# Attention and a gated MLP in one kernel: the opening reordered, weight joins and masks interleaved, the gate rewritten

## The chip, the cores and the metric

One core of a Trainium2 chip runs the whole program. The metric is device time in microseconds (us) from one launch to its end; the kernel before was timed three times, and one execution of it was profiled.

## The reference

Inputs are q, k, v of 4 batches, 8 heads, 768 positions, 64 dimensions, and two float64 weight matrices w_in (512 x 2048) and w_out (2048 x 512). Cut to what is computed:

```python
k_sum = k.reshape(B, H, nb, 32, D).max(axis=3)        # one summary key per block of 32
v_sum = v.reshape(B, H, nb, 32, D).mean(axis=3)
scores_l = scale * q @ k.T, masked to |i - j| < 16
scores_s = scale * q @ k_sum.T + log(32)
a = softmax(concat([scores_l, scores_s]))             # float32
x = (a @ concat([v, v_sum])) laid out as (3072, 512)
h = x @ w_in                                          # (3072, 2048)
g = where(h >= 1, h, where(h <= -1, 0, (h + 1)**2 / 4))
out = (g @ w_out).astype(float32)
```

## The kernel before

The 3072 rows of x are cut into 8 chunks of T = 384 (chunk c is half c % 2 of batch c // 2). For each chunk, attention runs over 4 head pairs p. Then the MLP runs over 16 blocks f of 128 hidden columns: `ff1` (F) makes h, the gate (G, H, I) makes t, `gate_high` (J) and `gate_rest` (O) split t into a high and a low part, and `ff2` (B) adds t @ w_out into three accumulators. Every product of the MLP is made of three matmuls on high and low halves, so F is 12 matmuls and B is 9.

A step has a letter and digits: `S13` is the scores of chunk 1, pair 3, `F0a2` the third part of ff1 of chunk 0, block 10. The attention letters are: r, k, q, y, v loads (raw keys, windowed keys, queries, raw values, windowed values); R, Y sums over blocks; K, C keys put together; S scores; M mask and row maximum; E exps; D reciprocals; N norms; T transposes and P their copies out of PSUM; Z, V, W the summary values; A the product with the values; X and L its high and low half. The dictionary `steps` maps them to functions.

The weights arrive as float64 words and are converted on the chip, in 16 pairs of pieces. Pair i holds w_out block i-1 and w_in block i+1 (pair 0: w_in blocks 0 and 1; pair 15: w_out blocks 14 and 15), so F of block f needs pair f-1 and B of block f needs pair f+1. A pair goes through w (fetch, 1 MB by two DMAs), a and b (two scalings on ScalarE), c (the join: shift, merge and add on VectorE through a PSUM bank, two halves of 512 columns), d (rounding to the high half) and e (the low half, on GpSimd). `HI_POOL` lists the pairs whose d runs on GpSimd; the others run on ScalarE.

The order is written out by hand for the opening only: the string `OPENING` is the order of all steps of chunk 0, of the attention of chunk 1 and of the start of chunk 2, and each engine gets its instructions in that order. After it a loop emits F, G, H, I, J, O of block f, one attention step of the next chunk, and B of block f-2 (LAG = 2); a scheduler places those. h has two PSUM banks (`ps_h`), so F of block f+2 can start only once the gate has read h of block f for the last time. All other PSUM tiles share six banks (`ps`), of which the accumulators hold three. Raw keys, raw values and joined weights share three buffers (`W_BUFS`). Loads are all issued in order by SyncE, with eight in flight.

Of the kernel before, what the change touches and what calls it, by code (L numbers as in the profile page):

```python
# [40 lines left out]
D001 T000 y01 Y01 a0 c00 c01 P000 N001 T001 P001 q01 S01 M011 M010 w1 a1 b1 y02 Y02 E011 D011 q02 S02 M021 M020 C03
q03 S03 v00 v01 V00 W00 v02 N011 k10 w2 E010 D010 N010 y03 Z01 Z02 V01 W01 V02 W02 c10 q10 q11 E021 D021 N021 E020
D020 N020 v03 C10 A00 T010 M030 P010 T011 M031 P011 v10 X00 L00 b2 Y03 E030 D030 N030 k11 C11 A01 T021 P021 X01 L01
v11 T020 P020 S10 M100 M101 q12 E031 D031 N031 E100 D100 N100 Z03 V03 W03 Z10 V10 W10 S11 q13 c11 E101 D101 N101 a2
A02 X02 T030 M110 T031 P031 M111 L02 E110 D110 E111 D111 N111 N110 k12 k13 C13 C12 P030 d0 d1 e0 e1 Z11 Z12 V11 W11
c20 c21 A03 X03 T101 P101 T100 L03 P100 w3 w4 a3 w5 b3 A10 X10 T110 P110 T111 P111 L10 v12 S12 M120 M121 q20 k20 S13
q21 E120 M131 M130 D120 N120 E121 k21 E131 D131 N131 D121 N121 V12 W12 F000 F001 F010 F011 F012 F002 F003 G00 F013
E130 D130 N130 G01 b4 c30 c31 H01 A11 T121 X11 L11 P121 T120 P120 I01 H00 I00 a4 a5 w6 w7 w8 a6 d2 e2 J00 O00 Z13 d3
e3 A12 T131 T130 P131 P130 c40 c41 d4 e4 F020 F030 F031 F032 F021 F022 F023 G02 F033 B00 b5 b6 v13 V13 W13 c50 v20
H02 I02 F040 F041 F042 F043 b7 b8 J01 O01 J02 O02 B01 B02 w9 b9 wa ba c51 c60 d5 e5 G03 H03 G04 c61 d6 H04 I04 F050  # L50
F051 F052 F053 I03 F060 F061 F062 a7 c70 c71 a8 a9 aa c80 F063 J03 O03 B03 G05 J04 O04 B04 G06 X12 e6 L12 d7 e7 H05
I05 F070 J05 F071 F072 F073 c81 d8 e8 H06 I06 J06 F080 F081 F082 F083 wb bb ab wc bc wd we wf bd be bf c90 c91 d9 ca0
A13 v21 O05 G07 H07 B05 O06 B06 G08 H08 ca1 e9 I07 F090 F091 F092 F093 I08 F0a0 F0a1 F0a2 F0a3 cb0 cb1 J07 O07 G09
B07 J08 O08 G0a B08 ac cc0 ad ae af H0a I0a da db ea F0b0 F0b1 eb F0b2 F0b3 H09 I09 F0c0 F0c1 F0c2 F0c3 cc1 cd0 cd1
J09 J0a O09 G0b O0a G0c H0b I0b B09 B0a H0c I0c dc ec F0d0 F0d1 F0d2 F0d3 dd ed F0e0 F0e1 F0e2 F0e3 ce0 ce1 cf0 J0b
J0c O0b O0c G0d H0d G0e H0e B0b B0c cf1 de df ee ef I0e F0f0 F0f1 F0f2 F0f3 I0d F100 F101 F102 J0d J0e X13 L13 F103
O0d O0e B0d G0f H0f I0f F110 F111 F112 F113 G10 H10 I10 F120 F121 F122 F123 B0e r20 R20 C20 y21 Y21 r21 R21 C21 J0f
J10 O0f G11 H11 B0f
# [8 lines left out]
def fused_kernel(ctx: ExitStack, tc: tile.TileContext, q2, kT, kwin, vT, vwin, w_in, w_out, mask, ident, out):  # L67
# [167 lines left out]
    def masks(c, p, j):  # L235
        e = es[c, p, j] = att.tile([P, NT, KA], F32, tag=f"e{j}", name=f"e{c}_{p}_{j}", bufs=E_BUFS)
        at = c % NHALF
        nc.vector.scalar_tensor_tensor(  # L238
            out=e, in0=s_pss[c, p][j][:, :NT * KA].rearrange("p (t n) -> p t n", n=KA), scalar=1.0 / math.sqrt(D),
            in1=mask_sb[:, at:at + NT], op0=ALU.mult, op1=ALU.add)  # L240
        dens[c, p, j] = att.tile([P, 2, NT], F32, tag=f"den{j}", name=f"den{c}_{p}_{j}")
        nc.vector.tensor_reduce(out=dens[c, p, j][:, 0], in_=e, axis=AX.X, op=ALU.max, negate=True)  # L242
# [214 lines left out]
```

## Time and profile before

| quantity | value |
| --- | --- |
| timed runs | 686.19 us median of 3 (685.07 to 1181.96) |
| profiled execution | 684.8 us |
| its span, first to last instruction | 683.0 us |
| TensorE (PE) busy | 641.8 us, 94% of the span |
| VectorE (DVE), ScalarE (ACT), GpSimd (POOL) busy | 338.6, 312.4, 260.2 us |
| mean granted TensorE clock | 0.988 |

The median and the profiled execution belong together; the 1181.96 us is one disturbed run. The span leaves 1.8 us of the profiled time outside. PE is the engine to watch: where it is busy all the time, no other engine matters. Some matmul records can be missing from a trace.

### The profile page before, as it was taken

The numbers are of one execution on the slowest core, as the hardware profiler recorded it, in microseconds if no ns is written. First come the engines' busy times: TensorE is split into PE (matmuls) and PEld (weight loads), VectorE is DVE, ScalarE is ACT, GpSimd is POOL, SyncE is SP. The second block draws the span as 40 slices with busy tenths as digits, with TensorE's granted clock in tenths as the row PEclk, the third lists the DMA queues.
The fourth block names the chain that finished last, engine by engine and source line by source line (L and its number), as shares of the span: only waits on it lengthen the run. The fifth ranks groups of instructions, "written<-read, shape, count | busy, mean of one in ns | idle before, by whom it ended". The sixth has DMA issues, their size and how long they took to land.

```text
span 683.0 us, 11672 instructions
## 1 busy us (share of the span) xinstructions
PE 641.8 (94%) x4448; PEld 558.9 (82%) x4448; DVE 338.6 (50%) x689; ACT 312.4 (46%) x825; POOL 260.2 (38%) x292
## 2 busy tenths in 40 slices
...
GB/s 309 324 242 343 341 166 0 50 139 151 64 63 55 118 63 46 62 119 191 63 45 37 155 46 63 63 65 246 31 50 62 93 63 18 1 1 46 1 1 46
DMA packets 31399, 69.05 MB, mean 101 GB/s; under 512 B 2928, under 2 KB 11376, under 8 KB 31344
## 3 DMA queue, kind: packets, MB, share of 16 engines
...
q8 instruction: 35, 0.57, 0.4%
...
HBM read 62.01 MB, written 6.29 MB: 100 GB/s over the span
## 4 chain that ended last, share of the span: by engine, by line
PE 82%; DMA 8%; DVE 6%; issue 2%; SPq 1%; ACT 1%; POOL 0%; DVEq 0%; POOLq 0%; ACTq 0%
PE acc L325 37%; PE h L294 35%; PE o_ps L273 4%; PE s_ps L231 3%; DMA raw<-in_w_out 3%; PE t_ps L262 3%; DMA raw<-in_w_in 3%; DVE c L127 2%; DMA first<-in_vT 1%; DVE c L125 1%; DVE w L129 1%; DMA first<-in_kT 1%; DVE t L300 1%; DVE t L306 1%; SPq L101 1%
## 5 line engine op out<-in xcount | busy, mean ns | idle before, releaser
L294 PE MATMUL h<-xhi,halves 128*128 128x384 f32 x1024 | 283.1, 339 | 7.0 <-DVE t L306 6.4
L316 POOL TENSOR_TENSOR glo<-t,ghi 128x384 fp32r<-128x384 f32 x128 | 129.7, 1016 | 329.3 <-PE acc L325 177.4
L325 PE MATMUL acc<-halves,ghi 128*128 128x512 f32 x768 | 240.6, 394 | 0.0
L294 PEld LDWEIGHTS h<-xhi,halves 128*128 128x128 f32 x1024 | 187.7, 188 | 14.4 <-DVE t L306 5.9
L303 ACT ACTIVATE t<-t,ones_half 128x384 f32<-128x384 f32 x128 | 78.6, 618 | 215.5 <-DVE t L300 215.3
L300 DVE TENSOR_SCALAR t<-h 128x384 f32<-128x384 f32 x128 | 70.6, 556 | 212.6 <-PE h L294 156.4
L294 PE MATMUL h<-xlo,halves 128*128 128x384 f32 x512 | 173.1, 338 | 0.0
L325 PEld LDWEIGHTS acc<-halves,ghi 128*128 128x128 f32 x768 | 144.8, 189 | 29.0
L325 PE MATMUL acc<-halves,glo 128*128 128x512 f32 x384 | 161.0, 419 | 1.3 <-POOL glo L316 1.3
L306 DVE TENSOR_TENSOR t<-h,t 128x384 f32<-128x384 f32 x128 | 70.8, 556 | 61.3 <-ACT t L303 61.0
L294 PEld LDWEIGHTS h<-xlo,halves 128*128 128x128 f32 x512 | 96.2, 188 | 5.1
L311 ACT CAST ghi<-t 128x384 fp32r<-128x384 f32 x128 | 65.2, 514 | 60.2 <-DVE t L306 57.1
L325 PEld LDWEIGHTS acc<-halves,glo 128*128 128x128 f32 x384 | 72.2, 188 | 20.8 <-issue 3.5
L247 ACT ACTIVATE e<-e,den 128x120 f32<-128x120 f32 x192 | 73.2, 383 | 17.7 <-DVE den L242 17.6
L257 POOL TENSOR_TENSOR e<-e,den 128x360 f32<-128x360 f32 x64 | 50.2, 790 | 29.6 <-DVE den L253 21.3
L266 ACT COPY pt<-t_ps 120x384 f32<-120x384 f32 x64 | 30.0, 474 | 48.9 <-PE t_ps L262 48.9
L142 POOL TENSOR_TENSOR halves<-w,halves 128x1024 fp32r<-128x1024 f32 x16 | 38.4, 2403 | 13.0 <-ACT halves L136 12.5
L231 PE MATMUL s_ps<-k,q 64*64 64x120 f32 x720 | 28.3, 294 | 12.0 <-DMA q<-in_q 6.8
L262 PE MATMUL t_ps<-ident_sb,e 128*120 128x128 f32 x192 | 30.8, 301 | 7.8 <-POOL e L257 7.8
L231 PEld LDWEIGHTS s_ps<-k,q 64*64 64x64 f32 x720 | 21.1, 147 | 19.6 <-POOL k L203 11.1
L238 DVE SCALAR_TENSOR_TENSOR e<-s_ps,mask_sb 128x360 f32<-128x360 f32 x64 | 33.4, 527 | 6.7 <-PE t_ps L262 3.0
L247 ACT ACTIVATION_READ_ACCUMULATOR e<-e,den 128x1 f32 x192 | 35.9, 187 | 0.0
...
## 6 DMA issues: line engine op xcount, KB each, us to landing
q<-in_q SPq DMA_DIRECT2D x30, 384.0 KB, 3.9
k<-in_kwin SPq DMA_DIRECT2D x28, 360.0 KB, 3.2
...
raw<-in_w_in SPq DMA_DIRECT2D x16, 512.0 KB, 10.3
raw<-in_w_out SPq DMA_DIRECT2D x16, 512.0 KB, 10.5
...
vraw<-in_vT SPq DMA_DIRECT2D x13, 384.0 KB, 3.5
kraw<-in_kT SPq DMA_DIRECT2D x13, 384.0 KB, 3.6
```

What stands on the lines that cost most here:

```text
L142: nc.gpsimd.tensor_tensor(out=lo, in0=converting[i].bitcast(F32), in1=hi.bitcast(F32), op=ALU.subtract)
L231: nc.tensor.matmul(s_ps[j][i * QB:(i + 1) * QB, t * KA:(t + 1) * KA], q_t[rows, blk, rows], k_t[rows, blk, :], start=True, stop=True)
L247: nc.scalar.activation(out=e[:, t, :], in_=e[:, t, :], func=AF.Exp, bias=nm[:, t:t + 1], scale=1.0, accum_out=den[:, t:t + 1])
L257: nc.gpsimd.tensor_tensor(out=e, in0=e, in1=den.unsqueeze(2).broadcast_to([P, NT, KA]), op=ALU.mult)
L262: nc.tensor.transpose(t_pss[c, p, j][:KA, t * P:(t + 1) * P], es[c, p, j][:, t, :], ident_sb)
L294: nc.tensor.matmul(hs[c, f][:, :T], weight["win", f][w][:, k * P:(k + 1) * P], x, start=(k == 0 and n == 0), stop=(k == NK - 1 and n == 2))
L300: nc.vector.tensor_scalar(out=ts[c, f], in0=hs[c, f][:, :T], scalar1=-1.0, scalar2=1.0, op0=ALU.max, op1=ALU.min)
L303: nc.scalar.activation(out=ts[c, f], in_=ts[c, f], func=AF.Square, bias=ones_half, scale=0.5)
L306: nc.vector.tensor_tensor(out=ts[c, f], in0=hs[c, f][:, :T], in1=ts[c, f], op=ALU.max)
L311: nc.scalar.copy(out=hi, in_=ts[c, f])
L316: nc.gpsimd.tensor_tensor(out=lo, in0=ts[c, f], in1=hi.bitcast(F32), op=ALU.subtract)
L325: nc.tensor.matmul(acc[c][i], a[:, rows], weight["wout", f][w], start=(f == 0 and n == 0), stop=(f == NF - 1 and n == 2))
```

## The change

Five things change, nothing in what is computed.

1. `convert_join` does both halves of a pair in one step. It takes two PSUM banks and issues shift, shift, merge, merge, add, add, where it issued shift, merge, add for one half and later the same for the other.
2. `masks` does both heads of a pair in one step: mask, mask, maximum, maximum instead of mask, maximum, mask, maximum.
3. The gate is written as min(r², max(h, 1)) with r = relu(h/2 + 1/2). The clip of h on DVE is gone; in its place ACT reads h from PSUM (relu with scale and bias), ACT squares, and DVE does max and min in one instruction.
4. `HI_POOL` holds all 16 pairs, so all d run on GpSimd.
5. `OPENING` is another order of the same steps.

```diff
-HI_POOL = [0, 2, 4, 6, 8, 10, 12, 14]
+HI_POOL = [0, 1, 2, 3, 4, 5, 6, 7, 8, 9, 10, 11, 12, 13, 14, 15]
...
 OPENING = """
-y00 Y00 r00 R00 K00 C00 q00 S00 r02 R02 m M001 M000 E000 Z00 r01 R01 w0 K01 C01 K02 C02 D000 N000 E001 r03 K03 R03 b0
+r03 r00 R00 r01 R01 K00 r02 q00 q01 m q02 q03 R03 K01 K02 C01 y02 C00 R02 C02 S00 S01 K03 C03 y00 w0 M00 E000 S02 M01
...
-        c_ps = ps.tile([P, DM], I32, tag="ps", name=f"c{i}_{part}")
-        nc.vector.tensor_scalar(out=c_ps, in0=top[:, cols], scalar1=3, scalar2=0x7FFFFFF8,
-                                op0=ALU.logical_shift_left, op1=ALU.bitwise_and)
-        nc.vector.scalar_tensor_tensor(out=c_ps, in0=top[:, cols], scalar=-0x80000000, in1=c_ps,
-                                       op0=ALU.bitwise_and, op1=ALU.bitwise_or)
-        nc.vector.tensor_tensor(out=w[:, cols], in0=c_ps, in1=low[:, cols], op=ALU.add)
+        c_ps = [ps.tile([P, DM], I32, tag="ps", name=f"c{i}_{part}") for part in range(2)]
+        cols = [slice(part * DM, (part + 1) * DM) for part in range(2)]
+        for part in range(2):
+            nc.vector.tensor_scalar(out=c_ps[part], in0=top[:, cols[part]], scalar1=3, scalar2=0x7FFFFFF8,
+                                    op0=ALU.logical_shift_left, op1=ALU.bitwise_and)
+        for part in range(2):
+            nc.vector.scalar_tensor_tensor(out=c_ps[part], in0=top[:, cols[part]], scalar=-0x80000000, in1=c_ps[part],
+                                           op0=ALU.bitwise_and, op1=ALU.bitwise_or)
+        for part in range(2):
+            nc.vector.tensor_tensor(out=w[:, cols[part]], in0=c_ps[part], in1=low[:, cols[part]], op=ALU.add)
...
-    def gate_clip(c, f):
+    def gate_half(c, f):
...
-        nc.vector.tensor_scalar(out=ts[c, f], in0=hs[c, f][:, :T], scalar1=-1.0, scalar2=1.0, op0=ALU.max, op1=ALU.min)
+        nc.scalar.activation(out=ts[c, f], in_=hs[c, f][:, :T], func=AF.Relu, bias=ones_half, scale=0.5)
...
-        nc.scalar.activation(out=ts[c, f], in_=ts[c, f], func=AF.Square, bias=ones_half, scale=0.5)
...
-        nc.vector.tensor_tensor(out=ts[c, f], in0=hs[c, f][:, :T], in1=ts[c, f], op=ALU.max)
+        nc.scalar.square(out=ts[c, f], in_=ts[c, f])
...
+        nc.vector.scalar_tensor_tensor(out=ts[c, f], in0=hs[c, f][:, :T], scalar=1.0, in1=ts[c, f], op0=ALU.max, op1=ALU.min)
```

How it moves instructions shows in three places. The first is VectorE in the middle of the weight conversion. The names are c (PSUM banks of a join, pair and half), w (the joined pair), h and t (gate of chunk 0, by block). Before:

```order
L300 TENSOR_SCALAR t0_7_1149<-h0_7_1055 128x384
L300 TENSOR_SCALAR t0_8_1171<-h0_8_1083 128x384
L125 TENSOR_SCALAR c10_1_1174<-raw10_941 128x512
L127 SCALAR_TENSOR_TENSOR c10_1_1174<-raw10_941,c10_1_1174 128x512
L129 ISA w10_1128<-raw10_941,c10_1_1174 128x1024
L306 TENSOR_TENSOR t0_7_1149<-h0_7_1055,t0_7_1149 128x384
L306 TENSOR_TENSOR t0_8_1171<-h0_8_1083,t0_8_1171 128x384
```

The clip (L300) of two blocks, half a join, and the maximum (L306) stand in one queue. VectorE now, at the same blocks:

```order
L308 SCALAR_TENSOR_TENSOR t0_6_1137<-h0_6_1020,t0_6_1137 128x384
L308 SCALAR_TENSOR_TENSOR t0_7_1145<-h0_7_1069,t0_7_1145 128x384
L123 TENSOR_SCALAR c10_0_1203<-raw10_1040 128x512
L123 TENSOR_SCALAR c10_1_1204<-raw10_1040 128x512
L126 SCALAR_TENSOR_TENSOR c10_0_1203<-raw10_1040,c10_0_1203 128x512
L126 SCALAR_TENSOR_TENSOR c10_1_1204<-raw10_1040,c10_1_1204 128x512
L129 ISA w10_1202<-raw10_1040,c10_0_1203 128x1024
L129 ISA w10_1202<-raw10_1040,c10_1_1204 128x1024
```

The clips have left VectorE, and no instruction of a join stands directly behind the one whose result it reads.

The second place is the load queue of SyncE ahead of the last raw values of chunk 0 (y03, here first11 loaded from in_vT). Before, from the second weight pair on:

```order
L181 DMA first12_89<-in_vT 128x768
L177 DMA first15_86<-in_q2 128x768
L177 DMA first14_87<-in_q2 128x768
L186 DMA v0_0_278<-in_vwin 96x768
L186 DMA v0_1_280<-in_vwin 96x768
L186 DMA first10_91<-in_vwin 96x768
L172 DMA k1_0_286<-in_kwin 128x720
L101 DMA raw2_288<-in_w_out 128x1024
L98 DMA raw2_288<-in_w_in 128x4x256
L181 DMA first11_90<-in_vT 128x768
```

It came right behind the third weight pair, and the keys of chunk 1, pair 1 five loads after it. SyncE now:

```order
L172 DMA k1_0_251<-in_kwin 128x720
L172 DMA k1_1_253<-in_kwin 128x720
...
L177 DMA q1_1_267<-in_q2 128x768
L100 DMA raw1_269<-in_w_out 128x1024
L97 DMA raw1_269<-in_w_in 128x4x256
L100 DMA raw2_272<-in_w_out 128x1024
L97 DMA raw2_272<-in_w_in 128x4x256
L100 DMA raw3_275<-in_w_out 128x1024
L97 DMA raw3_275<-in_w_in 128x4x256
L181 DMA first11_90<-in_vT 128x768
```

The keys of chunk 1, pair 1 have moved up, and y03 stands behind a fourth weight pair. On VectorE its sum Y03 now stands ahead of the low halves of pairs 1 and 2 and of the masks of chunk 1, pair 1:

```order
L207 TENSOR_REDUCE vs0_3_428<-first11_90 128x24
L286 TENSOR_TENSOR xlo0_1_432<-o_ps0_1_381,xhi0_1_431 128x384
L286 TENSOR_TENSOR xlo0_2_454<-o_ps0_2_440,xhi0_2_453 128x384
L254 TENSOR_SCALAR den1_0_1_426<-den1_0_1_426 128x3
L255 RECIPROCAL den1_0_1_426<-den1_0_1_426 128x3
L254 TENSOR_SCALAR den1_0_0_424<-den1_0_0_424 128x3
L255 RECIPROCAL den1_0_0_424<-den1_0_0_424 128x3
L239 SCALAR_TENSOR_TENSOR e1_1_0_519<-s_ps1_1_0_463,mask_sb_82 128x360
```

Before, Y03 was done well ahead of those masks. The third place is GpSimd in the weight conversion, where L134 is d, L142 is e and glo is O. Before:

```order
L142 TENSOR_TENSOR halves9_1126<-w9_1117,halves9_1126 128x1024
L316 TENSOR_TENSOR glo0_7_1217<-t0_7_1149,ghi0_7_1216 128x384
L316 TENSOR_TENSOR glo0_8_1232<-t0_8_1171,ghi0_8_1231 128x384
L134 CAST halves10_1257<-w10_1128 128x1024
L142 TENSOR_TENSOR halves10_1257<-w10_1128,halves10_1257 128x1024
L142 TENSOR_TENSOR halves11_1259<-w11_1207,halves11_1259 128x1024
```

The d of pairs 9 and 11 were on ScalarE. GpSimd now:

```order
L134 CAST halves9_1129<-w9_1120 128x1024
L142 TENSOR_TENSOR halves9_1129<-w9_1120,halves9_1129 128x1024
L318 TENSOR_TENSOR glo0_6_1149<-t0_6_1137,ghi0_6_1148 128x384
L318 TENSOR_TENSOR glo0_7_1167<-t0_7_1145,ghi0_7_1166 128x384
L134 CAST halves10_1241<-w10_1202 128x1024
L142 TENSOR_TENSOR halves10_1241<-w10_1202,halves10_1241 128x1024
L318 TENSOR_TENSOR glo0_8_1267<-t0_8_1220,ghi0_8_1266 128x384
```

Each e now has its d ahead of it on the same engine.

## Rows read from the trace of the kernel before

**Rows 1.** Busy time by stretch: start:end, length, engines with instruction counts, PEclk, DMA, GB/s

```profile
55.97:140.00 84.03, 73.74 (x429) 64.49 (x426) 74.68 (x131) 56.92 (x98) 59.90 (x42) 1.00 0.51 170
140.00:683.00 543.00, 538.74 (x3670) 471.81 (x3668) 223.81 (x470) 221.75 (x623) 176.46 (x209) 1.00 0.22 71
```

**Rows 2.** Waits of PE from 55.97 to 140: total us, times, longest

```profile
PE h L294 <- DVE t L306: 6.4, 5, 2.3
PE acc L325 <- POOL glo L316: 1.3, 2, 0.7
```

**Rows 3.** GpSimd timeline at 38.5: start, us, instruction, idle before and its releaser

```profile
38.54 0.30 POOL L203 COPY k<-ks 128x144 f32<-128x144 f32 x1 [4.11 <-DMA k<-in_kwin]
```

**Rows 4.** Chain that ended last: start us, us, what

```profile
42.79 0.54 DVE e L238
...
53.43 2.65 PE s_ps L231 x48
...
624.68 2.11 PE h L294 x12
628.89 2.11 PE h L294 x12
```

**Rows 5.** PE timeline: scores early, first F, first scores of chunk 2

```profile
33.61 0.85 PE L231 MATMUL s_ps<-k,q 64*64 64x120 f32 x24 [1.10 <-DVE den L253]
...
55.97 0.56 PE L294 MATMUL h<-xhi,halves 128*128 128x384 f32 x1
...
146.90 0.84 PE L231 MATMUL s_ps<-k,q 64*64 64x120 f32 x24
```

**Rows 6.** ACT timeline at 30.8

```profile
30.77 1.17 ACT L115 ACTIVATE raw<-raw 128x1024 int32<-128x1024 uint32 x1 [0.89 <-DMA raw<-in_w_in]
```

**Rows 7.** Busy time of the stretch 10 to 33 (last column: GB/s)

```profile
10.00:33.00 23.00, 13.21 (x140) 9.74 (x140) 21.09 (x46) 16.57 (x56) 9.82 (x20) 1.00 1.05 347
```

**Rows 8.** The page's DMA issues: count, KB each, median us to landing

```profile
q<-in_q SPq DMA_DIRECT2D x30, 384.0 KB, 3.9
k<-in_kwin SPq DMA_DIRECT2D x28, 360.0 KB, 3.2
...
raw<-in_w_in SPq DMA_DIRECT2D x16, 512.0 KB, 10.3
```

**Rows 9.** DVE timeline from 102.54 on, one half of a join and two maxima

```profile
102.54 0.68 DVE L125 TENSOR_SCALAR c<-raw 128x512 int32<-128x512 int32 x1
103.25 0.70 DVE L127 SCALAR_TENSOR_TENSOR c<-raw,c 128x512 int32<-128x512 int32 x1
103.98 0.69 DVE L129 CUSTOM_DVE_ANT_0 w<-raw,c 128x1024 uint16<-128x1024 uint16 x1
104.59 1.01 DVE L306 TENSOR_TENSOR t<-h,t 128x384 f32<-128x384 f32 x2
```

**Rows 10.** Groups from 55.97 to 140: count, busy us, mean ns, idle before

```profile
L142 POOL TENSOR_TENSOR halves<-w,halves 128x1024 fp32r<-128x1024 f32 x14 | 33.7, 2407 | 13.0 <-ACT halves L136 12.5
...
L316 POOL TENSOR_TENSOR glo<-t,ghi 128x384 fp32r<-128x384 f32 x15 | 15.0, 1024 | 3.7 <-ACT ghi L311 3.6
...
L115 ACT ACTIVATE raw<-raw 128x1024 int32<-128x1024 uint32 x12 | 13.2, 1145 | 3.4 <-DMA raw<-in_w_in 3.4
...
L303 ACT ACTIVATE t<-t,ones_half 128x384 f32<-128x384 f32 x17 | 10.1, 619 | 17.2 <-DVE t L300 17.1
L306 DVE TENSOR_TENSOR t<-h,t 128x384 f32<-128x384 f32 x17 | 8.9, 552 | 2.9 <-ACT t L303 2.9
L300 DVE TENSOR_SCALAR t<-h 128x384 f32<-128x384 f32 x17 | 8.8, 547 | 1.7 <-POOL glo L316 1.7
L311 ACT CAST ghi<-t 128x384 fp32r<-128x384 f32 x17 | 8.2, 513 | 4.9 <-DVE t L306 4.9
...
L134 POOL CAST halves<-w 128x1024 fp32r<-128x1024 f32 x7 | 7.3, 1041 | 0.3 <-DVE w L129 0.2
L247 ACT ACTIVATE e<-e,den 128x120 f32<-128x120 f32 x12 | 4.6, 383 | 1.7 <-DVE den L242 1.7
```

More of the change, by code (lines that the diff above doesn't have):

```diff
@@ L39 @@
 OPENING = """
-y00 Y00 r00 R00 K00 C00 q00 S00 r02 R02 m M001 M000 E000 Z00 r01 R01 w0 K01 C01 K02 C02 D000 N000 E001 r03 K03 R03 b0
[L41 to L58, printed above, removed]
+r03 r00 R00 r01 R01 K00 r02 q00 q01 m q02 q03 R03 K01 K02 C01 y02 C00 R02 C02 S00 S01 K03 C03 y00 w0 M00 E000 S02 M01
+S03 D000 N000 E011 D011 N011 E010 T000 P000 D010 N010 Y00 Z00 y01 E001 D001 N001 k10 k11 C11 a0 v00 v01 Y02 v02 C10
@@ new lines @@
+q10 q11 w1 w2 w3 y03 v03 Y01 b0 V00 T001 P001 W00 Z01 V01 Z02 V02 W02 W01 M02 E021 D021 N021 A00 T010 T011 X00 L00
+M03 P010 v10 P011 E020 D020 N020 c0 d0 E030 D030 N030 E031 D031 N031 A01 T021 T020 P021 S10 q12 M10 Y03 e0 X01 L01
+P020 a1 a2 a3 A02 X02 L02 E101 D101 N101 S11 q13 Z03 V03 W03 Z10 Z11 Z12 V10 W10 k12 C12 k13 C13 E100 D100 N100 r23
+b1 b2 T031 P031 T030 P030 M11 E111 c1 E110 D110 N110 D111 N111 A03 T101 P101 T100 X03 L03 d1 e1 P100 c2 d2 e2 v11 V11
+W11 w4 a4 w5 w6 A10 X10 v12 L10 T110 P110 T111 P111 b3 b4 b5 V12 W12 S12 S13 M12 E121 M13 D121 E120 D120 N120 k20
@@ new lines @@
+E131 N121 D131 N131 Z13 E130 D130 N130 c3 d3 w7 w8 F000 F010 F011 F001 F002 F003 G00 F012 H00 F013 G01 H01 I01 I00
+A11 T120 T121 P121 P120 A12 T130 X11 L11 T131 v13 v20 V13 X12 L12 P130 P131 W13 F020 F030 F031 F032 F033 F021 F022
+F023 e3 J00 J01 O00 O01 c4 d4 e4 a5 c5 d5 a6 a7 e5 a8 A13 X13 L13 B00 B01 G02 H02 I02 F040 F041 F042 F043 G03 H03 I03
+F050 F051 F052 F053 k21 b6 c6 b7 b8 c7 J02 J03 O02 B02 G04 H04 O03 B03 G05 H05 I05 F060 F061 F062 F063 q20 q21 w9 wa
+wb wc b9 ba a9 wd aa we wf d6 e6 d7 e7 I04 F070 F071 F072 F073 J04 J05 O04 O05 B04 B05 c8 d8 e8 c9 d9 e9 ab ac ad v21
@@ L59 @@
+F113 F123 r20 R20 C20 V20 Z23 W20 r21 R21 C21 r22 R22 J0f O0f G11 J10 O10 B0f
 """
```

36 lines of the change are left out of this document (20 added, 16 removed).

## The prediction

> **What bounds the kernel now.** I read the busy time by stretch first, with the lines of the opening as borders [rows 1]. The reader is to see where PE has gaps. From 140 us to the end of the span it is busy 538.7 of 543.0 us: it waits for nothing but the last store, so no edit to another engine can shorten this part. From the first F at 55.97 [rows 5] to 140 it is busy 73.7 of 84.0 us, so 10.3 us are idle. Before 55.97 PE does only small matmuls of attention, and what counts there is when the first F starts. The change can win in these two places only: an earlier first F, or fewer gaps behind it.
>
> The second view is PE's waits in that stretch [rows 2]: 6.4 of the 10.3 us are five waits for the last instruction of the gate on DVE, which frees the PSUM bank of h; 1.3 us are for O on GpSimd. The gate is late because DVE is full, busy 74.7 of 84.0 us [rows 1], and its instructions stand behind joins in one queue. So DVE bounds the conversion stretch, PE the rest.
>
> The third view is the chain that ended last, ahead of 55.97. At 38.54 GpSimd gets the windowed keys of chunk 1, pair 1 (k11), after 4.1 us of waiting for their load [rows 3]. Behind it come the scores, the masks of that pair at 42.79, its exps, then P03, A03, T10, A10, T11, and last the scores of pairs 2 and 3 at 53.43 [rows 4], right ahead of F. From those masks to the first F it is 55.97 - 42.79 = 13.2 us.
>
> **Start of the first F.** k11 moves up in the load queue and no longer holds anything. In its place y03 does: Y03 stands on DVE ahead of L01, L02, the reciprocals of S10 and the masks of pair 1, and y03 comes behind a fourth weight pair. When does it land? In the kernel before, the third weight pair landed at 30.77, since ScalarE waited for it until then [rows 6]. Counting both queues by the sizes of [rows 8], y03 now has in front of it and with it three more loads of 384 KB, one more weight pair of 2 x 512 KB and one more k of 360 KB than that pair had: 2536 KB, 2.6 MB. At the 347 GB/s of 10 to 33 us [rows 7] this takes 7.5 us: y03 lands at 38.3. Then Y03, L01 and L02 take some 2 us on DVE. Meanwhile ScalarE, which runs a for the fourth pair (landing just ahead of y03) and then X02, two times three exps of 0.38 us [rows 10] and small copies, is done with the exps of S10 at about 42; the masks of pair 1 follow at about 42.3. Behind them the chain is the one of before, 13.2 us with one whole join in it as before: the first F starts at about 55.0 to 55.5, say 55.0, 1 us earlier. Bounds: 51, if the loads run some 10% faster and ScalarE is not in the way; 58, if two of the many hops each lose a microsecond. The same scores, transposes and value products stand ahead of F in both orders (only Z13, one small matmul, moves ahead), so PE's remaining work is equal.
>
> **The join.** A join's instructions follow at 0.71 and 0.73 us where one reads what the last wrote, and the next independent one follows 0.61 us after the add [rows 9]. A pair costs 2 x (0.71 + 0.73 + 0.61) = 4.1 us now. Interleaved, nothing waits for its neighbour: 6 x 0.61 = 3.7 us, 0.44 less. From 55.97 to 140 there are 13 of the 16 pairs: 5.7 us of DVE. The masks gain some 0.2 us a pair by the same spacing, nothing that shows. The bounds are 0 and 5.7; I take the upper, since independent instructions of the same length stand in the row.
>
> The Trainium skill (VectorE: DVE Perf Modes, "The DRAIN you can't avoid") says that the next DVE instruction doesn't start before the pipe is empty, and that a chain costs the same with a semaphore after each instruction and without. By that rule the interleaving saves nothing and the joins stay at 4.1 us; the 0.61 against 0.72 us in [rows 9] speaks against it.
>
> **The gate.** The clip leaves DVE: 17 x 0.547 = 9.3 us of its busy time in the stretch, about 0.46 us each by the start-to-start time of two such instructions (1.01 for two, with 0.55 for one [rows 9, 10]), so 7.9 us. Max and min in one instruction cost what the maximum does, 0.55. On ScalarE the relu costs between the 0.51 of a plain cast and the 0.62 of the square with a bias [rows 10], 17 x 0.57 = 9.7 us; the square without a bias falls from 0.62 to about 0.51 (by L311), -1.8; seven d's of about 1.04 leave, -7.3. ScalarE ends where it was, 57 of 84 us. The gate passes through DVE's queue once and no longer twice.
>
> **The d on GpSimd.** Seven more of 1.04 us [rows 10], 7.3 us. In return e no longer waits for ScalarE's d, which is 12.5 us of GpSimd's idle time. A block then costs GpSimd d + e + O = 1.04 + 2.41 + 1.02 = 4.47 us, against 4.21 us of PE for F and B (628.89 - 624.68, [rows 4]). So GpSimd becomes the slowest engine of the conversion, by 0.26 us a block, 3.4 us in 13 blocks. Its lead takes some of it: three pairs are through e ahead of F, and F of block f needs only pair f-1. I put 1.5 us of stalls on it; bounds 0 and 3.4.
>
> **Gaps behind the first F.** DVE's work of the stretch falls from 74.7 to about 61 us while PE's stays 74, so DVE can keep up. One gap stays by order: F of block 2 needs I00, and on DVE I00 stands behind the masks of pairs 2 and 3 of chunk 1, the reciprocals of their twelve exps and the join c3. From the end of S12, 1.4 us ahead of F: masks 1.9, exps 12 x 0.38 = 4.6, reciprocals 0.3, c3 3.7, two I's 1.0; together 11.5, so block 2 starts 10.1 us after the first F. PE has F of blocks 0 and 1 (4.2) and two value products and two transposes (3.4 by the kind of [rows 5]) to fill it: 2.5 us idle. With 1.5 for GpSimd and 0.3 for hops, 4.3 us are left of 10.3: 6 us gained; bounds 2 and 8.3.
>
> **Sum.** Against the profiled execution: 684.8 - 1 - 6 = 677.8, its span 676.0. The median of the timed runs is 1.4 us above the profiled execution, so the median of the changed kernel may be 678 to 679; I say 678. Taking the good ends together, 684.8 - 5 - 8.3 = 671.5; the bad ends, 684.8 + 2 - 2 = 684.8. A measurement of this kernel can tell about 2%, 13.7 us, from no change; so this is within 2%.
>
> **Rivals.**
> *Everything in the opening falls into place:* y03 lands at 35, F starts at 50, and only 2 us of gaps stay: 684.8 - 6 - 8.3 = 670.5, or less if PE's clock is up sooner. For it: the sums above put all four compute engines at about 4 us a block. Against it: the load queue alone gives 38 for y03. 18%.
>
> *GpSimd takes DVE's place and gives it back:* if e's and O's come late from the first block on, the 3.4 us come in full, and a first F at 58 costs 2: 684.8 + 2 - 10.3 + 2.5 + 3.4 + 3 of hops = about 685. For it: GpSimd is above PE by these rows. Against it: e has a lead of three pairs when F starts. 14%.
>
> *The d's hold up DVE:* if each d on GpSimd kept one DVE instruction back for its 1.04 us, 7.3 us of DVE's 13.6 us would be lost again, and about half of the 6 us gained: 681. The Trainium skill (Perfetto Trace Analysis, "Optimizing Scalar/DVE Operations") warns that GpSimd and DVE share a read port, so that moving work between them might not help; by that rule it would come out so. In this trace d takes 1.04 us on GpSimd in a stretch where DVE is 89% busy [rows 1, 10], and a join's instructions keep their 0.7 us there [rows 9]. 6%.
>
> *ScalarE stalls the steady part:* the relu waits in ScalarE's queue behind the six exps of a head pair, 2.3 us, in 24 places of chunks 2 to 7. It decides from the point at which relu, square and I (1.6 us) and what stands ahead take longer than PE's cover, one F and two B's, 6.3 us: that is 4.7 us ahead of the relu, twice the exps. If other work adds that much and 1 us more, 24 x 1 = 24 us: 684.8 - 7 + 24 = 701.8; it is over 2% slower from 0.9 us on. Against it: ScalarE is 41% busy there [rows 1]. 4%.
>
> **How the numbers follow.** The forecast has 58%, with 671.5 to 685. The range runs from 670 to 687: it takes in the first rival's upper half and the second and third. Faster by over 2% (below 672.5) is most of the first rival: 0.18. Slower by over 2% is the fourth, and a little for an opening that goes wrong at once in several of its waits: 0.05. Within 2%: 0.77.
>
> **What would show it.** The joins' instructions 0.61 us apart; PE's waits for I down from 6.4 to about 3 us, with O and e on GpSimd in their place; GpSimd nearly without idle time from 60 to 120; Y03 starting at about 38 and behind it the masks of pair 1 at about 42; the first F at 55; the first scores of chunk 2, at 146.90 now [rows 5], at about 140; and 0 idle PE behind that. The scores of 24 matmuls took 0.85 us at 33.61 [rows 5] but 2.65 for two at 53.43 [rows 4], a slow clock for PE; if it is still slow in the first F, up to 4 us are lost. The prediction is wrong if the first F starts outside 51 to 58, or if gaps show behind the opening.

## The result and the profile after

The changed kernel takes 679.85 us (median of 4 runs, 678.68 to 680.34), the kernel before 685.63 in the same session: a ratio of 0.9917, 95% interval 0.9896 to 0.9938. So it is 0.8% faster, clear of no change by its interval and within 2%, and 1.9 us from the 678 predicted. The 685.63 counts the one disturbed execution of 1181.96 us; without it the median before is 685.07, and each difference from the changed kernel given below would be 0.6 us smaller. The profiled execution of the changed kernel took 680.34 us, the slowest of its four, with a span of 678.6 (before 684.8 and 683.0).

First the stretches, with the first F, the first scores of chunk 2 and the next scores of chunk 2 as borders. The columns are those of [rows 1]. Before:

```profile
55.97:146.90 90.93, 80.64 (x462) 70.32 (x458) 79.19 (x138) 58.80 (x102) 62.73 (x47) 1.00 0.48 161
146.90:158.92 12.02, 11.43 (x98) 9.31 (x98) 7.26 (x16) 6.91 (x22) 4.59 (x7) 1.00 0.81 274
158.92:683.00 524.08, 520.41 (x3540) 456.67 (x3539) 212.03 (x448) 212.96 (x597) 169.05 (x199) 1.00 0.21 66
```

After, and below it the 20 us in which the conversion is densest:

```profile
55.03:138.50 83.47, 80.75 (x463) 72.14 (x461) 69.50 (x123) 59.00 (x113) 70.52 (x55) 0.98 0.53 177
138.50:153.72 15.22, 12.91 (x97) 10.51 (x97) 4.62 (x13) 8.23 (x26) 3.98 (x6) 0.89 0.36 122
153.72:678.60 524.88, 520.51 (x3537) 456.68 (x3536) 147.04 (x338) 261.45 (x702) 169.00 (x198) 1.00 0.21 66
...
70.00:90.00 20.00, 20.00 (x122) 17.96 (x121) 20.00 (x35) 18.74 (x26) 19.68 (x16) 1.00 1.04 372
```

The lengths give the account: the first F is 0.94 us earlier, the conversion 7.46 us shorter at the same work of PE (80.6 and 80.8 us busy), the stretch between the two scores 3.20 us longer, the rest 0.80 longer; together 4.40, the difference of the spans. From 70 to 90 PE has no gap at all, while DVE and GpSimd are both full.

PE's waits from 55 to 140 us, which answer to [rows 2] (total, times, longest):

```profile
PE o_ps L275 <- ACT pt L268: 2.4, 1, 2.4
PE t_ps L264 <- POOL e L259: 0.2, 1, 0.2
```

The five waits for the gate on DVE are gone, and no wait for O or e stands in their place. PE's timeline of the changed kernel at the places of [rows 5], and the wait that grew:

```profile
55.03 0.42 PE L296 MATMUL h<-xhi,halves 128*128 128x384 f32 x1
...
64.10 1.25 PE L275 MATMUL o_ps<-pt,v 120*64 120x64 f32 x24 [2.39 <-ACT pt L268]
...
138.50 0.84 PE L231 MATMUL s_ps<-k,q 64*64 64x120 f32 x24
...
145.71 0.54 PE L264 MATMUL t_ps<-ident_sb,e 128*120 128x128 f32 x3 [2.31 <-POOL e L259]
```

DVE's timeline around y03, the masks of chunk 1, pair 1 and a join (compare [rows 4, 9]):

```profile
38.94 0.95 DVE L207 TENSOR_REDUCE vs<-first 128x24 f32<-128x768 f32 x1 [4.18 <-DMA first<-in_vT]
...
43.00 0.96 DVE L239 SCALAR_TENSOR_TENSOR e<-s_ps,mask_sb 128x360 f32<-128x360 f32 x2
...
44.74 1.28 DVE L123 TENSOR_SCALAR c<-raw 128x512 int32<-128x512 int32 x2
45.93 1.28 DVE L126 SCALAR_TENSOR_TENSOR c<-raw,c 128x512 int32<-128x512 int32 x2
47.12 1.28 DVE L129 CUSTOM_DVE_ANT_0 w<-raw,c 128x1024 uint16<-128x1024 uint16 x2
48.31 0.16 DVE L254 TENSOR_SCALAR den<-den 128x3 f32<-128x3 f32 x1
```

Two instructions start every 1.19 us, so a pair takes 48.31 - 44.74 = 3.57 us. The groups from the first F to the first scores of chunk 2, as in [rows 10]:

```profile
L142 POOL TENSOR_TENSOR halves<-w,halves 128x1024 fp32r<-128x1024 f32 x14 | 33.8, 2418 | 1.1
L318 POOL TENSOR_TENSOR glo<-t,ghi 128x384 fp32r<-128x384 f32 x17 | 17.1, 1021 | 1.4 <-ACT ghi L313 1.3
L134 POOL CAST halves<-w 128x1024 fp32r<-128x1024 f32 x13 | 13.6, 1043 | 2.7 <-DVE w L129 2.7
L302 ACT ACTIVATE t<-h,ones_half 128x384 f32<-128x384 f32 x19 | 11.0, 577 | 14.6 <-PE h L296 8.7 <-POOL glo L318 5.8
L308 DVE SCALAR_TENSOR_TENSOR t<-h,t 128x384 f32<-128x384 f32 x18 | 9.6, 557 | 5.6 <-ACT t L305 4.8 <-ACT ghi L313 0.8
```

The last field matters most. The gate's first instruction on ScalarE waits for PE and GpSimd now, never for DVE; before, the square waited 17.1 us for DVE's clip [rows 10].

### The profile page after: what moved, and what is told of

Same layout as the page of the kernel before. It is cut to its first block, busy times and chain, and to the rows that moved or that the text cites. A ratio compares the mean times of both kernels' runs of the same rounds, so it can differ in the third digit from the quotient of the medians.

```text
span 678.6 us, 11734 instructions
## 1 busy us (share of the span) xinstructions
PE 645.1 (95%) x4448; PEld 562.4 (83%) x4448; DVE 259.0 (38%) x561; ACT 363.1 (54%) x945; POOL 268.6 (40%) x300
## 4 chain that ended last, share of the span: by engine, by line
PE 80%; DMA 7%; ACT 4%; DVE 4%; POOL 2%; issue 2%; SPq 1%; POOLq 0%; ACTq 0%; DVEq 0%
PE acc L327 37%; PE h L296 34%; PE o_ps L275 3%; PE t_ps L264 3%; PE s_ps L231 2%; ACT e L249 2%; DMA vraw<-in_vT 2%; DMA v<-in_vwin 2%; DMA raw<-in_w_in 1%; DMA raw<-in_w_out 1%; DMA mask_sb<-in_mask 1%; DVE e L239 1%; SPq L100 1%; POOL glo L318 1%; DVE den L244 1%
## 5 line engine op out<-in xcount | busy, mean ns | idle before, releaser
L308 DVE SCALAR_TENSOR_TENSOR t<-h,t 128x384 f32<-128x384 f32 x128 | 70.8, 557 | 326.2 <-ACT t L305 302.0
L302 ACT ACTIVATE t<-h,ones_half 128x384 f32<-128x384 f32 x128 | 73.8, 577 | 190.2 <-PE h L296 178.3
L327 PEld LDWEIGHTS acc<-halves,glo 128*128 128x128 f32 x384 | 72.7, 189 | 19.2 <-issue 3.5
L305 ACT ACTIVATE t<-t 128x384 f32<-128x384 f32 x128 | 67.4, 527 | 3.0
L264 PE MATMUL t_ps<-ident_sb,e 128*120 128x128 f32 x192 | 33.1, 311 | 6.3 <-POOL e L259 5.4
L142 POOL TENSOR_TENSOR halves<-w,halves 128x1024 fp32r<-128x1024 f32 x16 | 38.6, 2411 | 1.2
L275 PEld LDWEIGHTS o_ps<-pt,v 120*64 120x64 f32 x720 | 25.8, 147 | 12.1 <-issue 6.1
L275 PE MATMUL o_ps<-pt,v 120*64 120x64 f32 x720 | 30.4, 237 | 3.9 <-ACT pt L268 3.2
## 6 DMA issues: line engine op xcount, KB each, us to landing
raw<-in_w_in SPq DMA_DIRECT2D x16, 512.0 KB, 10.3
```

Source lines behind the costliest of these rows:

```text
L264: nc.tensor.transpose(t_pss[c, p, j][:KA, t * P:(t + 1) * P], es[c, p, j][:, t, :], ident_sb)
L275: nc.tensor.matmul(o_pss[c, p][j * D:(j + 1) * D, cols], v_ts[c, p][:KA, blk, j * D:(j + 1) * D], pts[c, p, j][:KA, cols], start=True, sto ...
L302: nc.scalar.activation(out=ts[c, f], in_=hs[c, f][:, :T], func=AF.Relu, bias=ones_half, scale=0.5)
L305: nc.scalar.square(out=ts[c, f], in_=ts[c, f])
L308: nc.vector.scalar_tensor_tensor(out=ts[c, f], in0=hs[c, f][:, :T], scalar=1.0, in1=ts[c, f], op0=ALU.max, op1=ALU.min)
L327: nc.tensor.matmul(acc[c][i], a[:, rows], weight["wout", f][w], start=(f == 0 and n == 0), stop=(f == NF - 1 and n == 2))
```

## Experiments

Times differ by some tenths of a per cent between sessions, so "against the changed kernel" below is the difference of two differences: (a kernel minus the kernel before of its session) minus (679.85 - 685.63 = -5.8 us).

**order_only** is the new order with all instructions of the kernel before.

The edit is to the kernel before; c and M are written as two steps each, as it wants them.

```diff
-y00 Y00 r00 R00 K00 C00 q00 S00 r02 R02 m M001 M000 E000 Z00 r01 R01 w0 K01 C01 K02 C02 D000 N000 E001 r03 K03 R03 b0
+r03 r00 R00 r01 R01 K00 r02 q00 q01 m q02 q03 R03 K01 K02 C01 y02 C00 R02 C02 S00 S01 K03 C03 y00 w0 M000 M001 E000
...
```

> The new order with the old instructions: joins and masks not interleaved, clip on VectorE, every second d on ScalarE. Theory 1 (relief of VectorE is what empties the queue ahead of I): VectorE gets back 17 clips at 0.46 us and 13 joins at 0.44 us, 13.6 us between the first F and the first scores of chunk 2; PE waits for the gate again, 6 to 10 us of gaps, the first F at about 55.5: 684 to 689 us. Theory 2 (the order alone earns the gain): 680 us, within 1 us of the changed kernel, with gaps of some 3 us.

Measured: 715.81 us against 684.62, ratio 1.0447 (1.0425 to 1.0469): 31 us slower than before, far outside what either theory gave. The two largest waits of ScalarE from 55 to 150 us in it:

```profile
ACT t L303 <- DVE t L300: 25.8, 9, 7.5
ACT halves L136 <- DVE w L129: 15.4, 3, 5.8
```

The square waits for the clip and the d for the join, both on DVE, and what stands behind them in ScalarE's queue waits too.

**instr_only** is the old order with all new instructions; the edit is to the changed kernel, as in all that follow.

```diff
-r03 r00 R00 r01 R01 K00 r02 q00 q01 m q02 q03 R03 K01 K02 C01 y02 C00 R02 C02 S00 S01 K03 C03 y00 w0 M00 E000 S02 M01
+y00 Y00 r00 R00 K00 C00 q00 S00 r02 R02 m M00 E000 Z00 r01 R01 w0 K01 C01 K02 C02 D000 N000 E001 r03 K03 R03 b0 D001
...
```

> The old order with the new instructions: interleaved joins and masks, the new gate, all d on GpSimd. Theory 1: VectorE is relieved just the same, so PE's waits for I shrink from 6.4 to 2 us or less, the first F stays at 55.5 to 56: 679 to 682 us. Theory 2 (the order alone earns the gain): 685 to 687 us, with the 10 us of gaps of before, since places in the queues and not busy time make the waits.

Measured: 688.94 us, ratio 1.0076 (1.0054 to 1.0099): slower than before. The stretch from its first F to its first scores of chunk 2, and the path into its longest gap (ScalarE, DVE and PE timelines):

```profile
55.73:153.34 97.61, 85.49 (x462) 75.99 (x458) 65.93 (x119) 60.57 (x113) 70.33 (x56) 0.93 0.45 149
```

```profile
72.30 0.58 ACT L301 ACTIVATE t<-h,ones_half 128x384 f32<-128x384 f32 x1 [2.38 <-PE h L295]
72.78 2.16 ACT L113 ACTIVATE raw<-raw 128x1024 int32<-128x1024 uint32 x2
74.95 0.27 ACT L214 ACTIVATE v<-vs_ps 24x128 f32<-24x128 f32 x1
75.24 0.53 ACT L304 ACTIVATE t<-t 128x384 f32<-128x384 f32 x1
...
75.25 0.69 DVE L122 TENSOR_SCALAR c<-raw 128x512 int32<-128x512 int32 x1 [3.36 <-ACT v L214]
...
78.24 0.55 DVE L307 SCALAR_TENSOR_TENSOR t<-h,t 128x384 f32<-128x384 f32 x1
...
78.94 0.48 PE L295 MATMUL h<-xhi,halves 128*128 128x384 f32 x1 [4.10 <-DVE t L307]
```

DVE is relieved (65.9 us busy of 97.6, where it had 79.2 of 90.9) and PE is idle 12.1 us all the same, more than before. The old order puts two scalings between relu and square, and the join on DVE, held for 3.4 us by what the profile puts down to the copy at 74.95, stands ahead of I. What waits there is the second half of the join. A join now takes two PSUM banks at once, and the copy reads from one of the same six banks, so the second bank may be what it waits for; no run tests this. So theory 1, the relief of DVE by itself, falls; with order_only, theory 2 falls as well. What is left is a third theory: the gain is the fit between order and instructions. Each queue is worked off in its order, an instruction that waits holds all behind it, and the new order leaves no room for an instruction that waits for another engine in the middle of a busy queue. If so, undoing one instruction change under the new order should cost more than its busy time, and the waits should name the queue.

**old_gate** is the changed kernel with the gate of before.

```diff
-        nc.scalar.activation(out=ts[c, f], in_=hs[c, f][:, :T], func=AF.Relu, bias=ones_half, scale=0.5)
+        nc.vector.tensor_scalar(out=ts[c, f], in0=hs[c, f][:, :T], scalar1=-1.0, scalar2=1.0, op0=ALU.max, op1=ALU.min)
...
-        nc.scalar.square(out=ts[c, f], in_=ts[c, f])
+        nc.scalar.activation(out=ts[c, f], in_=ts[c, f], func=AF.Square, bias=ones_half, scale=0.5)
```

> The changed kernel with the old gate: clip on VectorE, square with bias on ScalarE, maximum on VectorE. Theory 1: 7.9 us of work come back to VectorE behind the first F, and the gate passes its queue twice: PE waits for the gate 3 to 7 us more, 683 to 687 us. Theory 2 (order alone): 680 us.

Measured: 691.28 us, ratio 1.0098 (1.0080 to 1.0116), 12.4 us above the changed kernel. ScalarE's largest wait and PE's largest from 55 to 150 us:

```profile
ACT t L305 <- DVE t L302: 40.1, 15, 5.8
...
PE o_ps L275 <- ACT pt L268: 6.4, 1, 6.4
```

The 6.4 us (2.4 in the changed kernel) are not a wait of F for the gate: the square of block 0 waits 4.9 us for a clip that stands behind the join c3 on DVE, and the copies of chunk 1's transposes (pt) stand behind the square. Theory 1's own waits came as well: F waits for the gate on DVE five times, 5.0 us together, where the changed kernel has no such wait. The whole loss is more than theory 1 allowed for.

**plain_join** takes the two halves of a join one after the other, in the same two banks.

```diff
-        for part in range(2):
             nc.vector.scalar_tensor_tensor(out=c_ps[part], in0=top[:, cols[part]], scalar=-0x80000000, in1=c_ps[part],
...
-        for part in range(2):
             nc.vector.tensor_tensor(out=w[:, cols[part]], in0=c_ps[part], in1=low[:, cols[part]], op=ALU.add)
```

> The changed kernel with the two halves of a join one after the other, in the same two banks: shift, merge, add, shift, merge, add. Both theories expect a start-to-start time of 4.1 us a pair against 3.6 now. Theory 1: 13 pairs x 0.5 = 6 us more on VectorE, partly in its slack of that stretch: 1 to 4 us more, 681 to 684 us. Theory 2: 680 us, with the half microsecond a pair in VectorE's idle time.

Measured: 683.76 us, ratio 0.9993 (0.9977 to 1.0010), 4.9 us above the changed kernel. DVE's timeline in it:

```profile
81.22 0.69 DVE L123 TENSOR_SCALAR c<-raw 128x512 int32<-128x512 int32 x1
81.95 0.69 DVE L125 SCALAR_TENSOR_TENSOR c<-raw,c 128x512 int32<-128x512 int32 x1
82.68 0.69 DVE L127 CUSTOM_DVE_ANT_0 w<-raw,c 128x1024 uint16<-128x1024 uint16 x1
83.28 0.69 DVE L123 TENSOR_SCALAR c<-raw 128x512 int32<-128x512 int32 x1
```

A half takes 83.28 - 81.22 = 2.06 us, a pair 4.1 against 3.57 interleaved. From one start to the next it is 0.73 us where an instruction reads the last result, 0.60 where it does not. The Trainium skill (VectorE: DVE Perf Modes, "The DRAIN you can't avoid") has eight copies take the same time with a semaphore after each as with one after the last only; read as the prediction weighed it, that interleaving saves nothing, this does not hold for these instructions. Theory 1 is borne out: F waits for the gate on DVE again, five times and 3.6 us together, and the loss is somewhat above its 1 to 4 us.

**half_pool** puts d of the odd pairs back on ScalarE.

```diff
-HI_POOL = [0, 1, 2, 3, 4, 5, 6, 7, 8, 9, 10, 11, 12, 13, 14, 15]
+HI_POOL = [0, 2, 4, 6, 8, 10, 12, 14]
```

> The changed kernel with d of the odd pairs on ScalarE as before. GpSimd, which has next to no idle time from 70 to 110 us, loses 7 x 1.04 = 7.3 us of work there, and its e waits for ScalarE's d again. Theory A (GpSimd's saturation is covered by the lead of e, and d there takes a wait away): 0 to 3 us slower than the changed kernel, 680 to 683 us, with waits of e for d and of F for e. Theory B (all d on GpSimd costs what a block lasts above PE's): 1 to 3 us faster, 677 to 679 us.

Measured: 697.78 us, ratio 1.0194 (1.0178 to 1.0210), 19.2 us above the changed kernel; theory A gave at most 3, and B a gain. ScalarE's largest wait:

```profile
ACT halves L136 <- DVE w L129: 12.1, 3, 4.5
```

The timeline at the first of these three waits, ScalarE and then PE:

```profile
67.31 1.04 ACT L136 CAST halves<-w 128x1024 fp32r<-128x1024 f32 x1 [4.48 <-DVE w L129]
68.26 0.57 ACT L302 ACTIVATE t<-h,ones_half 128x384 f32<-128x384 f32 x1
...
70.31 0.84 ACT L268 COPY pt<-t_ps 120x384 f32<-120x384 f32 x2
...
71.21 1.55 PE L275 MATMUL o_ps<-pt,v 120*64 120x64 f32 x24 [7.89 <-ACT pt L268]
```

ScalarE stands idle for 4.5 us at d of pair 3 until the join c3 is done, while h of blocks 0 and 1 has been complete since 61.7 us (the last matmul of F, 61.34 + 0.33), and the copies wait behind their relus. PE waits 7.9 us at this one place, 2.4 in the changed kernel. The Trainium skill says that the queues of ScalarE, VectorE and GpSimd are strictly first in, first out (PSUM — Partial Sum Buffer, "Engine vs sequencer instructions"); these rows agree. PE's other waits from 55 to 140 us are 5.6 us for the gate, 3.0 for e and 1.4 for O; the changed kernel has none of these.

**late_d** asks whether it is the place of d or its time; its edit is to half_pool.

```diff
-... N130 c3 d3 w7 w8 F000 ... F023 e3 J00 ... c5 d5 a6 a7 e5 a8 A13 X13 ... c9 d9 e9 ab ac ad v21 G06 H06 I06 F080 G07 H07 J06
+... N130 c3 w7 w8 F000 ... F023 d3 e3 J00 ... c5 a6 a7 a8 A13 X13 d5 e5 ... c9 ab ac ad v21 G06 H06 I06 F080 G07 H07 d9 e9 J06
```

> As half_pool (d of the odd pairs on ScalarE), with three of them written later: d of pairs 3, 5 and 9, which made ScalarE wait 12.1 us for VectorE's joins with the relus and copies standing behind them, now stand behind those relus and copies, ahead of their e. ScalarE does as much work as in half_pool. Theory A (the place of d in ScalarE's queue, not its time, cost the 18 us): most of it comes back, 682 to 687 us. Theory B (ScalarE's time for d, or e waiting for d, costs it): 694 to 698 us.

Measured: 688.39 us, ratio 1.0061 (1.0037 to 1.0085): 9.5 of the 19.2 us come back from three moved d's, with the same work on every engine (the two e's that move along pass no other step of GpSimd). From 55 to 150 us, ScalarE's wait for joins and GpSimd's for d:

```profile
ACT halves L136 <- DVE w L129: 1.1, 1, 1.1
...
POOL halves L142 <- ACT halves L136: 13.3, 5, 5.1
```

The first fell from 12.1 us; the second was 5.6 in two waits in half_pool. So a d on ScalarE is either early, and holds the gate, or late, and holds e. The time lies between the two theories' ranges; the place of these three in the queue is half of the 19 us. PE still waits 2.6 us for e and 2.6 for O, so the hand-over to e on GpSimd goes with what is left, which was not taken apart further.

The remaining runs try the places where the changed kernel still waits.

**handover** moves the start of chunk 2 forward, against the 2.31 us at 145.71.

```diff
-... V21 W21 Z22 F110 ... C20 V20 Z23 W20 ... O0f G11 J10 O10 B0f
+... V21 W21 F110 ... C20 V20 W20 ... O0f G11 J10 O10 H11 I11 S20 M20 B0f E200 E201 D200 N200 D201 N201
```

> The end of the opening rearranged: I of the first block of chunk 1's second step, then the scores and masks of chunk 2's first pair, and its exps, reciprocals and norms stand in the written order, right behind the last O of the opening and ahead of the last B; the sums Z22 and Z23 move behind. Theory A (the 2.31 us that PE waits for the norm at 145.71, with the slow clock behind it, is where 3.2 us of the gain were given back): the wait shrinks to under 0.7 us, the slow clock there goes, 2 to 4 us faster than the changed kernel, 676 to 678 us. Theory B (the wait follows the windowed keys of chunk 2, pair 2, which stand ahead of the norm on GpSimd and land at 144.5): it stays at about 2 us, 679 to 680 us.

Measured: 678.93 us, ratio 0.9921 (0.9902 to 0.9940), 0.3 us from the changed kernel, theory B's time. Yet its profile shows half of what A said, in PE's timeline:

```profile
142.65 0.54 PE L264 MATMUL t_ps<-ident_sb,e 128*120 128x128 f32 x3 [1.25 <-POOL e L259]
```

The wait is down from 2.31 to 1.25, not to under 0.7; the granted clock of 140 to 150 us is 1.00 and not 0.83, and the span is 675.2. That execution was the fastest of its six (677.0 to 681.5), so the profile alone would have said 3 us where the runs say none that can be told. Nor does the clock show what the edit did: in exps_first, the next run, the wait is 2.34 and the clock is 1.00 all the same.

**exps_first** takes scalings out of the way of chunk 1's exps, against the 2.39 us at 64.10.

```diff
-... w4 a4 w5 ... P111 b3 b4 b5 V12 ... X12 L12 P130 ... e3 J00 J01 O00
+... w4 b3 a4 w5 ... P111 V12 ... X12 b4 L12 P130 ... e3 J00 J01 b5 O00
```

> ScalarE's b of pairs 4 and 5 moved behind the exps of chunk 1, pairs 2 and 3, and b of pair 3 ahead of a of pair 4. Theory A (the gap of 2.39 us that PE has at 64.10 ends with these exps and copies, which stand behind 3.3 us of scalings): the gap falls to 0 to 1 us and the clock stays high behind it, 1.5 to 4 us faster than the changed kernel, 676 to 678.5 us; the joins of pairs 4 and 5 come later by 1 to 3 us, without a wait of F. Theory B (VectorE's join c3 and the masks end last there, not ScalarE): the gap stays within 0.5 us of 2.39, 679 to 681 us.

Measured: 678.96 us, ratio 0.9920 (0.9903 to 0.9937), 0.4 us from the changed kernel. In its profile the gap is still 1.90 us: ScalarE now waits 2.20 us for the masks on DVE instead of working on scalings. Theory B's mechanism.

**two** is both of these together.

> The edits of handover and exps_first together. Theory A (the two gaps are independent, and their medians each show about 1 us): 677 to 678 us. Theory B (what one stretch gives is lost in the gaps of the steady part, or the gap at 64 ends with I of block 0 behind the join c3 whatever ScalarE does): 679 to 680 us.

Measured: 679.06 us, ratio 0.9912 (0.9891 to 0.9932). Theory B's time. Its first F started at 56.90, that of exps_first at 55.21, although the order is the same up to there: y03 landed later, so that its sum Y03 started at 40.92 and not at 39.69, and the masks of pair 1 at 44.98 and not at 43.75. So one profile of this opening can't tell differences under some 2 us.

**gate_first** adds an earlier gate of block 0 to two.

```diff
-... N130 c3 d3 w7 ... G00 F012 H00 F013 G01 H01 I01 I00 A11 T120 T121 P121 P120 A12
+... N130 w7 ... G00 F012 H00 F013 I00 A11 T120 T121 P121 P120 G01 H01 I01 c3 d3 A12
```

> As two, with the join c3 behind I of blocks 0 and 1 on VectorE, and the copies P12 ahead of relu and square of block 1 on ScalarE. Theory A (the gap of PE at 64 ends with I of block 0 behind c3): I of block 0 ends at about 62.7 and not at 66, the gap falls from 1.9 to about 1 us or less: 1 us faster than two, 676 to 677 us; joins come 1.3 us later, without a wait. Theory B (VectorE has no time to lose from 70 to 92 us): the 1.3 us come back as waits of F for I or for e, 678 to 680 us.

Measured: 679.94 us, ratio 0.9933 (0.9914 to 0.9952), theory B's side. PE's timeline:

```profile
62.72 0.92 PE L275 MATMUL o_ps<-pt,v 120*64 120x64 f32 x24 [1.12 <-ACT pt L268]
...
73.25 0.80 PE L327 MATMUL acc<-halves,glo 128*128 128x512 f32 x1 [2.64 <-POOL glo L318]
```

The gap fell to 1.12 us as meant. But I of block 1 keeps c3 until 64.21, where it began at 61.61 in exps_first, and these 2.6 us pass through d and e of pair 3 to O of block 0 on GpSimd (72.19 after 69.61), which stands behind them: PE waits the whole 2.64 us for it, nine microseconds later.

**y03_early** moves the load of y03 ahead of two weight pairs.

```diff
-... w1 w2 w3 y03 v03 ... a1 a2 a3 A02 ... r23 b1 b2 ... e1 P100 c2
+... w1 y03 v03 w2 w3 ... a1 A02 ... r23 b1 a2 b2 ... e1 P100 a3 c2
```

> The raw values y03 and the windowed values v03 ahead of the weight pairs 2 and 3 in the load queue, and ScalarE's a of pairs 2 and 3 later. Theory A (the landing of y03 sets the first F, through the masks of chunk 1, pair 1): 2 MB less ahead of it, Y03 starts at 33 to 35 and not at 38.9, the masks of pair 1 at 39 to 41, the first F at 51 to 53 and not at 55.03; 2 to 4 us faster, 676 to 678 us. Theory B (the exps on ScalarE or PE's own small matmuls at the slow clock end last by then): the first F within 1 us of 55.0, 679 to 681 us.

Measured: 680.53 us, ratio 0.9945 (0.9925 to 0.9964), 1.9 us above the changed kernel. The first F is at 57.57, later than either theory said, because another load had become late. GpSimd's timeline:

```profile
48.45 0.30 POOL L203 COPY k<-ks 128x144 f32<-128x144 f32 x1 [6.60 <-DMA k<-in_kwin]
...
50.12 2.28 POOL L259 TENSOR_TENSOR e<-e,den 128x360 f32<-128x360 f32 x3
```

The norms that the chain to the first F needs stand behind the keys of chunk 1, pairs 2 and 3.

**keys_later** is two with y03_early, and these keys behind the norms.

```diff
-... k12 C12 k13 C13 E100 ... N111 A03
+... k12 k13 E100 ... N111 C12 C13 A03
```

> As two, with the edit of y03_early, and with the keys C12 and C13 behind the norms of pairs 0 and 1 of chunk 1 on GpSimd, since in y03_early these norms waited 6.6 us behind C12 for the keys k12. Theory A (that wait alone kept y03_early from an earlier first F): the masks of pair 1 at 40.7, the first F at 52.5 to 53.5, 2 us faster than two, 675 to 677 us. Theory B (weight pair 3 and the keys k12 now land too late for the rest): the first F at 55 or later, 678 us or more.

Measured: 678.45 us, ratio 0.9915 (0.9891 to 0.9939): no difference from the changed kernel, between the two theories. The masks of pair 1 start at 38.90, 4.1 us earlier than in the changed kernel, and the first F at 54.23, 0.8 us earlier. ScalarE's timeline shows what took a part of the other 3.3 us:

```profile
38.48 1.10 ACT L114 ACTIVATE raw<-raw 128x1024 int32<-128x1024 uint32 x1
39.48 1.11 ACT L109 ACTIVATE raw<-raw 128x1024 f32<-128x1024 f32 x1
40.50 1.10 ACT L114 ACTIVATE raw<-raw 128x1024 int32<-128x1024 uint32 x1
...
42.23 0.41 ACT L249 ACTIVATE e<-e,den 128x120 f32<-128x120 f32 x1
```

The exps of pair 1, last in these lines, stand behind three scalings and start 2.7 us earlier than in the changed kernel (44.92), not 4.1: 1.4 us are lost here. Where the other 1.9 us go was not taken apart.

No version here can be told from the changed kernel on the faster side.

## Why the prediction was right, and which of its terms were not

**What bounds the kernel.** Right in its place: all that was won or lost lies ahead of the steady part, which changed by 0.8 us. Too narrow in its cause: "DVE bounds the conversion stretch" is only half of it, since instr_only relieves DVE and gets slower. Under the new order DVE's time does count: F's waits for the gate come back with 3.6 us in plain_join and 5.0 in old_gate.

**Start of the first F.** Predicted 55.0, measured 55.03; y03 at 38.3 and 38.94, the masks at 42.3 and 43.00. That the sum comes out to 0.03 us is luck. Two misses offset each other: the masks were 0.7 us late, and from them to F it took 12.0 us, not the 13.2 of before. And with this order up to F the profiles of the changed kernel, handover and old_gate have the first F at 55.03 to 55.39, those of exps_first and two, where only a scaling moved, at 55.21 and 56.90; so the 0.94 us against the one profile of before are not shown to be a gain. The path holds: in these five profiles Y03 starts anywhere from 38.67 to 40.92, and the masks 4.1 us behind it each time. But y03 sets the first F only within about 1 us: in keys_later, with the masks 4.1 us earlier, F came 0.8 us earlier, with ScalarE's scalings in the way.

**The gaps.** Predicted 4.3 of 10.3 us left, measured 83.47 - 80.75 = 2.7. The gap behind F of block 1 was predicted at 2.5 us and is 2.39, but the wait that ends it in the trace is another than the one forecast. PE waits at 64.10 for the copies pt, which stand on ScalarE behind twelve exps and the first two gates; the forecast had F of block 2 wait for I of block 0. The two I's run from 65.56 to 66.57 and F of block 2 starts at 66.47, without a wait in the profile, so both were due at nearly the same time. The 1.5 us for GpSimd did not come: it is 98% busy from 70 to 90 and PE waits for neither e nor O. The first scores of chunk 2, predicted at about 140, stand at 138.50.

**The terms behind that sum** were sized as busy time, and the runs priced them otherwise. Taken out one at a time under the new order, the join is worth 4.9 us (the upper bound of 5.7 was taken), the gate 12.4 (7.9 of DVE's time) and the d on GpSimd 19.2, where the step put a cost of 1.5. That is the term that failed: it counted 7.3 us of GpSimd's work and e's idle time, and left out that a d on ScalarE holds the relus and copies behind it. The rows had a hint of this kind: the 17.1 us that ScalarE's square waited for the clip [rows 10] were read as idle time of an engine off the path. The three add up to 36.5 us, and order_only, which takes out all three and the masks, is 37.0 us above the changed kernel; each of these figures is good to 1 or 2 us only. In the old order the same instructions together cost 4.3 us. So the total was near and its split was not: none of the 6 us belongs to an edit by itself.

**The total, and luck in it.** Against the profiled execution 7.0 us were forecast and 4.5 came. The gaps gave 7.6 us for the 6 forecast; behind them 3.20 and 0.80 us were lost where the forecast had nothing. That the median lies only 1.9 us from 678 comes of misses that run against each other.

**Not foreseen:** 3.20 us lost between the first scores of chunk 2 and the next, 1.72 of them idle (12.02 - 11.43 before, 15.22 - 12.91 after) and 1.48 a longer busy time at a granted clock of 0.89. The prediction had named no idle PE behind these scores as a sign of being right, and gaps behind the opening as a sign of being wrong; this gap of 2.31 us lies at the opening's end, so the first sign failed. The 1.48 us are not fixed by the order: exps_first and y03_early, with the same order there, have the gap (2.34 and 2.28 us) and a clock of 1.00, and take 13.67 and 13.62 us from these scores to the next, not 15.22. In the profile the keys of chunk 2, pair 2 and the masks behind two I's stand ahead of the norms; handover shortened that wait, but its runs don't confirm a gain, so what it is worth stays open.

**The rivals.** Everything in the opening falls into place: no, Y03 started at 38.94 and F at 55.03, not at 35 and 50. The d's hold up DVE: no. The join keeps 1.19 us for two with GpSimd full, and d and e take 1043 and 2418 ns (1041 and 2407 before). A stall of ScalarE in the steady part: no, the rest is 0.80 us longer. GpSimd in DVE's place: not in the changed kernel; but in gate_first a join that came 2.6 us late was passed on in full, so there was no slack left in that queue.
